# Transposing attention probabilities with the DMA engines instead of TensorE in a fused attention and feed-forward kernel

## The chip, the core and the metric

The kernel runs on one core of a Trainium2 chip. The core has five engines with an instruction queue each: TensorE (PE in the profile; its weight loads are PEld), VectorE (DVE), ScalarE (ACT), GpSimd (POOL) and SyncE (SP), which here issues the DMA transfers. An engine takes its instructions in order, and waits for other engines and for transfers by semaphores. The metric is the device time of one execution in microseconds.

## The reference

Attention over 4 batches of 8 heads, 768 positions and 64 numbers per head; each position sees the first `n_global` = 8 keys and the `n_local` = 96 keys that end with itself, with a bias that falls with the distance. The heads' outputs, side by side, are the 3072 rows of 512 numbers that go into a gated feed-forward layer with 1536 inner columns.

```python
scores = scale * np.matmul(q, k.transpose(0, 1, 3, 2))
keep = is_global | is_local
scores = np.where(keep, scores + bias[None], -1000000000.0)
a = np.exp(scores - np.max(scores, axis=-1, keepdims=True))
a = a / (np.sum(a, axis=-1, keepdims=True) + 1e-09)
x = np.matmul(a, v)                       # then heads side by side
gate = 1.0 / (1.0 + np.exp(-(x @ w_gate)))
out = (gate * (x @ w_val)) @ w_out
```

## The kernel before

The 3072 rows are worked on in 8 blocks of 384 rows (3 tiles of 128), two per batch; `PAIR` is 1, so blocks 0 and 1 come first in a prologue, and "the third block" is block 2. The feed-forward layer of a block takes 12 slices, one for each 128 of the 1536 inner columns, 96 slices in all. A slice (`ff_in`, then `ff_out` of the slice before) is: 12 matmuls into the bank ps_g (L537), a tanh on ACT that makes the gate (L545), 12 matmuls into ps_u, a multiplication on DVE that empties ps_u (L554), the split of the product into a rounded part hh (ACT) and a rest hl (DVE), and 9 output matmuls into ps_o (L577). A number is multiplied as a rounded part plus a rest; so the slice's output weights are split too, w2h on ACT (L217) and w2l on POOL (L180).

While the feed-forward layer of a block runs, the attention of the next block is put between its instructions. An attention item is one tile of 128 rows for one pair of heads: 12 per block, 4 pairs (steps) of 3 tiles. An item goes through these stages:

- S, `scores`: matmuls into ps_s (L387 for blocks 2 and on), bias and minimum on DVE (L406), exponential on ACT (L419); the result, 128 rows by 2 heads by 256 key columns in 32 bits, is a tile work. At the first tile of a batch the rows have 128 key columns.
- T, `normalise` and `transposes`: DVE divides by the sums (L434 to L438), PE transposes 128x128 pieces into the bank ps_t (L449; 4 pieces, 2 at the first tile of a batch), and one copy brings them to the SBUF tile pT (ACT at L457, for two thirds of block 0 DVE at L455).
- V, `values`: for both pairs of two steps together, matmuls of pT with v (L476), after which ACT and DVE write the split x of the next block (xh L518, xl L519).

A list of events gives each stage its slice: S at slice u, T at u + 1, V at u + 1 of the last tile of a step, with u spread over the slices of the block before. Events of kind 0 run ahead of `ff_in`, of kind 1 in its middle, behind the gate, of kind 2 behind it, ahead of `ff_out`. A scheduler then orders each engine's queue by its own estimates of time; `issue_after` holds one instruction behind another of the same engine. The inputs of a step are loaded two steps ahead (L301 to L325), into buffers that the step before last must have freed; SP issues loads and output stores (L600) in one order.

Of the kernel before, what the change touches and what calls it, by code (L numbers as in the profile page):

```python
# [8 lines left out]
F32 = mybir.dt.float32  # L9
# [3 lines left out]
I16 = mybir.dt.int16  # L13
# [6 lines left out]
P = 128  # L20
# [8 lines left out]
def attn_moe_kernel(ctx, tc, qT, kT, v, n_global, n_local, wg, wv, wo, out, B, H, S, D):  # L29
    nc = tc.nc  # L30
    DM = H * D
    NC = DM // P
    NF = wo.shape[0] // P
# [2 lines left out]
    TB = 3  # L36
    NB = TB * P
    WORKB = 4
    OSTB = 4
    PTB = 3  # L40
    QB = 2
    SCALE = 1.0 / float(D) ** 0.5
# [13 lines left out]
    spool = inner.enter_context(tc.tile_pool(name="spool", bufs=2))  # L56
# [3 lines left out]
    late = {}  # L60

    def issue_after(later, earlier):
        tc.add_manual_dep(
            later.ins,
            earlier.ins.name,
            mybir.DependencyInfo(mybir.DependencyClass.NoSync, mybir.DependencyReason.DATA),
            reason="issue order",
        )
# [5 lines left out]
    words = cpool.tile([P, 2, 2], I32, name="words")  # L74
# [74 lines left out]
    last_gate = []  # L149
# [118 lines left out]
    PAIR = 1  # L268
# [15 lines left out]
    steps = {}  # L284
# [66 lines left out]
    def bank(*names):  # L351

        i = turns.get(names, 0)
        turns[names] = i + 1
        name = names[i % len(names)]
        pool = {"ps_s": ps_a, "ps_t": ps_a, "ps_v": ps_a, "ps_g": ps_gv, "ps_u": ps_gv}.get(name, ps_o)
        return pool.tile([P, 4 * P], F32, name=name)
# [82 lines left out]
    def transposes(bi, s, t):  # L440
        st = steps[bi, s]
        b, t0, nt = blocks[bi]
        n = 1 if t0 + t == 0 else 2
        sb, _ = st.pop(("s", t))
        pt = bank("ps_t", "ps_o0") if bi < PAIR else bank("ps_t")
        pt = pt.rearrange("p (c x) -> p c x", c=4)
        for j in range(2):
            for c in range(n):
                nc.tensor.transpose(pt[:, n * j + c], sb[:, j, c * P:(c + 1) * P], ident)  # L449
        if bi > PAIR and s % 2:  # L450
            pT = late["pool"].tile([P, 4, P], F32, name="pT2", bufs=PTB)
        else:
            pT = spool.tile([P, 4, P], F32, name="pT", tag="pT", bufs=PTB)
        if bi < PAIR and t > 0:
            nc.vector.tensor_copy(pT[:, 0:2 * n], pt[:, 0:2 * n])  # L455
        else:
            nc.scalar.copy(pT[:, 0:2 * n], pt[:, 0:2 * n])  # L457
        st["pT"][t] = pT

    def values(bi, pairs):  # L460
        b, t0, nt = blocks[bi]
        n = nt * P

        lead = None
        avs = []
        for s in reversed(pairs):
            st = steps.pop((bi, s))
            shared = bi == PAIR or (bi > PAIR and s % 2)
            av = ps_a.tile([P, 4 * P], F32, name="ps_t" if shared else "ps_v")
            avs.append((s, av, st))  # L470
            for t in reversed(range(nt)):
                vts = (st["v1"],) if t0 + t == 0 else (st["v0"], st["v1"])
                m = len(vts)
                for c, vt in enumerate(vts):
                    for j in range(2):
                        ins = nc.tensor.matmul(  # L476
                            av[j * D:(j + 1) * D, t * P:(t + 1) * P],
                            vt[:, t, j * D:(j + 1) * D],
                            st["pT"][t][:, m * j + c],
                            start=(c == 0),  # L480
                            stop=(c == m - 1),
                        )
                        if lead is not None:
                            issue_after(ins, lead)
                        lead = ins
        for s, av, st in avs:
            pair_out(bi, s, av, st)
# [33 lines left out]

    outs = {}
    hs = {}

    UNSPLIT = 8

# [34 lines left out]
    def ff_out(bi, f):  # L561
        b, t0, nt = blocks[bi]
        if bi < PAIR and f < UNSPLIT:
            (h,) = hs.pop((bi, f))
            parts = ((h, w2f[f].bitcast(F32)),)
        else:
            hh, hl = hs.pop((bi, f))
            held, wh, wl = w2[0]
            assert held == f
            parts = ((hh, wl), (hh, wh), (hl, wh))  # L570
        if f == 0:
            outs[bi] = [ps_o.tile([P, DM], F32, name=f"ps_o{i}") for i in range(nt)]
        end = f == NF - 1 and bi == nblk - 1
        before = None
        for t in range(nt):
            for k, (ht, wt) in enumerate(parts):
                ins = nc.tensor.matmul(  # L577
                    outs[bi][t],
                    ht[:, t * P:(t + 1) * P],
                    wt,  # L580
                    start=(f == 0 and k == 0),
                    stop=(f == NF - 1 and k == len(parts) - 1),
                )

                if end and before is not None:
                    issue_after(ins, before)
                before = ins
        if f == NF - 1:
            for t in range(nt):
                ot = late["pool"].tile([P, DM], F32, name="ost", bufs=OSTB)  # L590
                if t == nt - 1 and end:
                    half = slice(0, DM // 2), slice(DM // 2, DM)
                    nc.scalar.activation(ot[:, half[0]], outs[bi][t][:, half[0]], AF.Copy, scale=0.5)  # L593
                    nc.vector.tensor_scalar(ot[:, half[1]], outs[bi][t][:, half[1]], 0.5, None, op0=ALU.mult)  # L594
                elif t == 1 and end:
                    nc.vector.tensor_scalar(ot, outs[bi][t], 0.5, None, op0=ALU.mult)
                else:
                    nc.scalar.activation(ot, outs[bi][t], AF.Copy, scale=0.5)
                row = b * S + (t0 + t) * P
                nc.sync.dma_start(out[bass.ds(row, P), :], ot)  # L600
# [8 lines left out]
    for bi, (b, t0, nt) in enumerate(blocks):  # L609
        items = [(s, t) for s in range(NPAIR) for t in range(nt)]  # L610
        if bi < PAIR:
            w = (-200, -80)
        elif bi == PAIR:
            w = (0, NF - LEAD)
        else:

            w = ((bi - 1) * NF - (LEAD if bi > PAIR + 1 else 0), bi * NF - LEAD)
        for k, (s, t) in enumerate(items):
            u = w[0] + k * (w[1] - w[0]) // len(items)

            lag = AHEAD if bi < PAIR else 1
            events.append((u, 0, "S", bi, s, t))
            events.append((u + lag, 1, "T", bi, s, t))
            if t == nt - 1:
                events.append((u + lag * (1 if bi >= PAIR else 2), 1 if bi == PAIR else 2, "V", bi, s, t))
    order = sorted(range(len(events)), key=lambda i: (events[i][0], events[i][1], i))
    events = [events[i] for i in order]

# [9 lines left out]
    def run(kind, bi, s, t):  # L638
        if kind == "S":
            if t == 0 and (bi, s) == (0, 0):  # L640
                ready_step((bi, s))
            scores(bi, s, t)
            if t == blocks[bi][2] - 1:
                i = all_steps.index((bi, s))
                if i + 1 < len(all_steps) and all_steps[i + 1] != (PAIR + 1, 0):
                    ready_step(all_steps[i + 1])
        elif kind == "T":
            normalise(bi, s, t)
            transposes(bi, s, t)
        else:  # L650
            if bi <= PAIR:
                values(bi, (s,))
            elif s % 2:
                values(bi, (s - 1, s))
# [18 lines left out]
        pos += 1  # L673
    prev = None
    for u, (bi, f) in enumerate(seq):
        group = {0: [], 1: [], 2: []}
        while pos < len(events) and events[pos][0] <= u:
            group[events[pos][1]].append(events[pos][2:])
            pos += 1
        if bi == 0:  # L680
            conv_until(2 * f)
        if u == NF - LEAD:
            conv_until(len(conv))
            cstack.close()
            late["pool"] = inner.enter_context(tc.tile_pool(name="late", bufs=1))
            load_step(PAIR + 1, 0)
            ready_step((PAIR + 1, 0))
        for e in group[0]:
            run(*e)
        if bi == 0:  # L690
            conv_step()

        def mid(es=group[1]):
            for e in es:
                run(*e)
            if bi == 0:
                conv_step()

        ff_in(bi, f, mid)
        for e in group[2]:  # L700
            run(*e)
        if prev is not None:
            ff_out(*prev)
        if bi < PAIR:
            conv_until(2 * f + 1)
        if bi >= PAIR or f >= UNSPLIT:
            split_w2(f, u == len(seq) - 1)
        prev = (bi, f)
# [149 lines left out]
```

## Time and profile before

| | |
|---|---|
| median of 3 runs | 769.31 us (768.39 to 769.98) |
| the profiled execution, its time | 771.78 us |
| its span, first to last instruction | 770.0 us |
| mean granted TensorE clock | 0.990 |
| PE busy, weight loads | 755.6 us (98%), 682.3 us (89%) |
| DVE, ACT, POOL busy | 405.6, 408.8, 213.2 us |
| DMA moved | 57.01 MB, mean 74 GB/s |

In a row of groups, the parts are: line, engine, operation, tile written <- tiles read, shape, count, then total busy us and mean ns of one, then the idle time of the engine ahead of them with what ended it. In a row by stretches, they are: the stretch in us, its length, then busy us and count for PE, PEld, DVE, ACT and POOL (or those that the chosen tile has), the granted clock, the busy share of the DMA engines and GB/s. In a row in order of time: start, duration, engine, line, operation, tiles, count, and in brackets the idle time ahead. A row of DMA issues ends with KB each and the median us from issue to landing. A row of waits gives who waited for whom: us in total, times, longest.

### The profile page before, as it was taken

The numbers are of one execution on the slowest core, as the hardware profiler recorded it, in microseconds if no ns is written. First come the engines' busy times: TensorE is split into PE (matmuls) and PEld (weight loads), VectorE is DVE, ScalarE is ACT, GpSimd is POOL, SyncE is SP. The second block draws the span as 40 slices with busy tenths as digits, with TensorE's granted clock in tenths as the row PEclk, the third lists the DMA queues.
The fourth block names the chain that finished last, engine by engine and source line by source line (L and its number), as shares of the span: only waits on it lengthen the run. The fifth ranks groups of instructions, "written<-read, shape, count | busy, mean of one in ns | idle before, by whom it ended". The sixth has DMA issues, their size and how long they took to land. (4 is left out here: it accounts for less than half of the span.)

```text
span 770.0 us, 12641 instructions
## 1 busy us (share of the span) xinstructions
PE 755.6 (98%) x4661; PEld 682.3 (89%) x4661; DVE 405.6 (53%) x1085; ACT 408.8 (53%) x944; POOL 213.2 (28%) x164
## 2 busy tenths in 40 slices
PE   8999999999999999999999999999999999999996
PEld 5767678899999999999999999999999999999995
DVE  6789887556445555554565544454654565221111
ACT  4689876645546555553556554464555555432222
POOL 5424234332313323221232322222221222112222
PEclk7999999999999999999999999999999999999998
DMA  8768553403022121122113110221211200000001
GB/s 255 218 214 263 179 194 91 120 14 92 8 73 77 34 75 33 39 83 58 37 37 92 60 54 20 68 74 37 71 37 42 78 25 17 1 10 33 1 0 46
DMA packets 66982, 57.01 MB, mean 74 GB/s; under 512 B 17248, under 2 KB 59232, under 8 KB 66912
## 3 DMA queue, kind: packets, MB, share of 16 engines
q1 hardware_dynamic: 66912, 56.12, 24.7%
q8 instruction: 39, 0.64, 0.3%
q14 instruction: 31, 0.25, 0.1%
HBM read 49.81 MB, written 6.29 MB: 73 GB/s over the span
## 5 line engine op out<-in xcount | busy, mean ns | idle before, releaser
L180 POOL TENSOR_TENSOR w2l<-w2f,w2h 128x512 fp32r<-128x512 f32 x87 | 114.0, 1310 | 414.3 <-ACT w2h L217 406.3
L554 DVE SCALAR_TENSOR_TENSOR work<-work,ps_u 128x384 f32<-128x384 f32 x88 | 48.7, 553 | 216.7 <-PE ps_u L537 207.8
L537 PE MATMUL ps_u<-xh,w1l 128*128 128x384 f32 x384 | 134.4, 350 | 0.0
L537 PE MATMUL ps_g<-xh,w1l 128*128 128x384 f32 x384 | 131.3, 342 | 1.2 <-ACT work L545 1.2
L537 PE MATMUL ps_g<-xl,w1h 128*128 128x384 f32 x384 | 130.4, 339 | 0.7 <-DVE xl L519 0.7
L537 PE MATMUL ps_u<-xl,w1h 128*128 128x384 f32 x384 | 129.9, 338 | 0.0
L537 PE MATMUL ps_g<-xh,w1h 128*128 128x384 f32 x384 | 129.9, 338 | 0.0
L537 PE MATMUL ps_u<-xh,w1h 128*128 128x384 f32 x384 | 129.9, 338 | 0.0
L557 ACT ACTIVATE hh<-work 128x384 fp32r<-128x384 f32 x88 | 46.0, 522 | 128.0 <-DVE work L554 128.0
L419 ACT ACTIVATE work<-work,nms 128x256 f32<-128x256 f32 (+1 forms) x192 | 92.0, 481 | 27.4 <-DVE nms L406 27.0
L577 PE MATMUL ps_o<-w2l,hh 128*128 128x512 f32 x261 | 104.7, 401 | 0.7 <-POOL w2l L180 0.6
L577 PE MATMUL ps_o<-w2h,hh 128*128 128x512 f32 x261 | 102.7, 394 | 0.0
L577 PE MATMUL ps_o<-w2h,hl 128*128 128x512 f32 x261 | 102.6, 394 | 0.0
L217 ACT ACTIVATE w2h<-w2f 128x512 fp32r<-128x512 f32 x87 | 54.9, 631 | 89.6 <-PE ps_o L577 88.6
L180 DVE TENSOR_TENSOR hl<-work,hh 128x384 fp32r<-128x384 f32 x88 | 69.3, 788 | 28.9 <-ACT hh L557 28.7
L537 PEld LDWEIGHTS ps_g<-xh,w1l 128*128 128x128 f32 x384 | 72.3, 188 | 5.2 <-issue 2.6
L537 PEld LDWEIGHTS ps_g<-xl,w1h 128*128 128x128 f32 x384 | 72.2, 188 | 3.0 <-DVE xl L519 1.1
L537 PEld LDWEIGHTS ps_u<-xh,w1l 128*128 128x128 f32 x384 | 72.3, 188 | 1.1 <-issue 0.2
L537 PEld LDWEIGHTS ps_u<-xl,w1h 128*128 128x128 f32 x384 | 72.4, 189 | 0.5
L537 PEld LDWEIGHTS ps_g<-xh,w1h 128*128 128x128 f32 x384 | 72.2, 188 | 0.7
L537 PEld LDWEIGHTS ps_u<-xh,w1h 128*128 128x128 f32 x384 | 72.2, 188 | 0.2 <-issue 0.2
L406 DVE CUSTOM_DVE_ANT_0 work<-ps_s,tab 128x256 f32<-128x256 f32 x136 | 52.7, 420 | 25.4 <-PE ps_s L387 25.0
(131 smaller groups left out, 1169.1 us busy)
## 6 DMA issues: line engine op xcount, KB each, us to landing
qr<-in_qT SPq DMA_DIRECT2D x56, 192.0 KB, 3.3
kr<-in_kT SPq DMA_DIRECT2D x32, 192.0 KB, 2.6
v<-in_v SPq DMA_DIRECT2D x32, 192.0 KB, 3.1
raw<-in_w_gate SPq DMA_DIRECT2D x12, 512.0 KB, 4.2
raw<-in_w_val SPq DMA_DIRECT2D x12, 512.0 KB, 5.8
raw<-in_w_out SPq DMA_DIRECT2D x12, 512.0 KB, 3.8
out<-ost SPq DMA_DIRECT2D x24, 256.0 KB, 2.2
v<-in_v SPq DMA_DIRECT2D x16, 144.0 KB, 2.7
```

The costliest lines, as they stand in the source:

```text
L180: eng.tensor_tensor(out, a, b, op=ALU.subtract)
L217: ins = nc.scalar.activation(hi, w, AF.Copy)
L406: ins = nc.vector.tensor_tensor_reduce(sb[:, j, :w], ps[j][:, :w], (tabs0 if zero else tabs)[2 * s + j], -SCALE, 3.0e38, op0=ALU.add, op1= ...
L419: ins = nc.scalar.activation(sb[:, j, :w], sb[:, j, :w], AF.Exp, scale=-1.0, bias=nm[:, j:j + 1], accum_out=sm[:, j:j + 1])
L537: nc.tensor.matmul(ps[:, :n], wt[f][:, i, c], xt[:, c, :n], start=(k == 0), stop=(k == 3 * NC - 1))
L554: nc.vector.scalar_tensor_tensor(a[:, :n], a[:, :n], 1.0, pss[1][:, :n], op0=ALU.add, op1=ALU.mult)
L557: nc.scalar.activation(hh[:, :n], a[:, :n], AF.Copy)
L577: ins = nc.tensor.matmul(outs[bi][t], ht[:, t * P:(t + 1) * P], wt, start=(f == 0 and k == 0), stop=(f == NF - 1 and k == len(parts) - 1),)
```

## The change

From block 2 on, T no longer uses PE. `transposes_by_dma` takes the 32-bit probabilities as 16-bit halves: two DVE copies (L467) put the lower halves and the upper halves of all pieces side by side in one tile `halves` (one buffer, 128 x 1024, or 128 x 512 at the first tile of a batch), and a transposing DMA on SP's queue (L469) writes `turned` (two buffers). A new stage J, `join`, runs one slice later: an ACT copy (L482) writes the lower halves and a DVE copy (L483) the upper halves into pT, each held behind that slice's gate tanh on its list of events. V moves to u + 2 of the last tile, behind `ff_out`, and its matmuls are held behind the last output matmul. The events of block 2 spread over 9 slices in place of 10, and those of the later blocks start and end one slice earlier. The output tiles `ost` have 3 buffers in place of 4. The values that are computed stay the same.

```diff
-    OSTB = 4
+    OSTB = 3
...
         sb, _ = st.pop(("s", t))
+        if bi > PAIR:
+            st["pT"][t] = transposes_by_dma(s, n, sb)
+            return
         pt = bank("ps_t", "ps_o0") if bi < PAIR else bank("ps_t")
...
-        if bi > PAIR and s % 2:
-            pT = late["pool"].tile([P, 4, P], F32, name="pT2", bufs=PTB)
-        else:
-            pT = spool.tile([P, 4, P], F32, name="pT", tag="pT", bufs=PTB)
+        pT = spool.tile([P, 4, P], F32, name="pT", tag="pT", bufs=PTB)
...
+    def transposes_by_dma(s, n, sb):
+
+        m = 2 * n
+        halves = late["pool"].tile([P, 2 * 4 * P], I16, name="halves")[:, 0:2 * m * P]
+        words = sb[:, :, 0:n * P].bitcast(I16).rearrange("p j (x h) -> p j x h", h=2)
+        for h in range(2):
+            dst = halves[:, h * m * P:(h + 1) * m * P].rearrange("p (j x) -> p j x", j=2)
+            nc.vector.tensor_copy(dst, words[:, :, :, h])
+        turned = late["pool"].tile([P, 2 * 4, P], I16, name="turned", bufs=2)[:, 0:2 * m]
+        nc.sync.dma_start_transpose(turned, halves)
+        return turned
+
+    def join(bi, s, t):
+        st = steps[bi, s]
+        turned = st["pT"][t]
+        m = 2 if blocks[bi][1] + t == 0 else 4
+        if s % 2:
+            pT = late["pool"].tile([P, 4, P], F32, name="pT2", bufs=PTB)
+        else:
+            pT = spool.tile([P, 4, P], F32, name="pT", tag="pT", bufs=PTB)
+        words = pT[:, 0:m].bitcast(I16).rearrange("p c (x h) -> p c x h", h=2)
+
+        issue_after(nc.scalar.copy(words[:, :, :, 0], turned[:, 0:m]), last_gate[-1])
+        issue_after(nc.vector.tensor_copy(words[:, :, :, 1], turned[:, m:2 * m]), last_gate[-1])
         st["pT"][t] = pT
...
-        lead = None
+        lead = last_out[-1] if bi > PAIR else None
...
+        last_out[:] = [before]
...
-            w = ((bi - 1) * NF - (LEAD if bi > PAIR + 1 else 0), bi * NF - LEAD)
+            w = ((bi - 1) * NF - (LEAD + 1 if bi > PAIR + 1 else 0), bi * NF - LEAD - 1)
...
+            if bi > PAIR:
+                events.append((u + 2 * lag, 1, "J", bi, s, t))
             if t == nt - 1:
-                events.append((u + lag * (1 if bi >= PAIR else 2), 1 if bi == PAIR else 2, "V", bi, s, t))
+                after, kind = (2, 2) if bi < PAIR else (1, 1) if bi == PAIR else (2, 3)
+                events.append((u + after * lag, kind, "V", bi, s, t))
...
         if prev is not None:
             ff_out(*prev)
+        for e in group[3]:
+            run(*e)
```

How the queues change is seen in three places. First TensorE, in a slice of the next to last block (w1l_153 and w1h_141 are the weights of one slice). Before, between the gate matmuls and the output matmuls, and the same once more behind the output matmuls:

```order
L537 MATMUL ps_g<-xh,w1h_141 128x384
L449 MATMUL ps_t<-ident,work 128x128 x2
L577 MATMUL ps_o_6696<-w2l,hh 128x512
L577 MATMUL ps_o_6696<-w2h,hh 128x512
L577 MATMUL ps_o_6696<-w2h,hl 128x512
```

Now, at the same place:

```order
L564 MATMUL ps_g<-xh,w1h_141 128x384
L604 MATMUL ps_o_6804<-w2l,hh 128x512
L604 MATMUL ps_o_6804<-w2h,hh 128x512
L604 MATMUL ps_o_6804<-w2h,hl 128x512
L604 MATMUL ps_o_6805<-w2l,hh 128x512
```

The transposes are gone from the queue, here and behind the output matmuls, and nothing stands in their place. The value matmuls, which stood ahead of a slice's output matmuls every sixth slice, now stand behind them.

Second VectorE, from the multiplication that empties ps_u to the next one, in a slice without a split of k. Before:

```order
L554 SCALAR_TENSOR_TENSOR work<-work,ps_u 128x384
L406 ISA work,nms<-ps_s,tab_127 128x256
L406 ISA nms 128x1
L406 ISA work,nms<-ps_s,tab_128 128x256
L406 ISA nms 128x1
L180 TENSOR_TENSOR hl<-work,hh 128x384
L434 TENSOR_SCALAR sm<-sm 128x2
L436 RECIPROCAL rc<-sm 128x2
L438 TENSOR_SCALAR work<-work,rc 128x256 x2
L554 SCALAR_TENSOR_TENSOR work<-work,ps_u 128x384
```

Now:

```order
L581 SCALAR_TENSOR_TENSOR work<-work,ps_u 128x384
L406 ISA work,nms<-ps_s,tab_125 128x256
L406 ISA nms 128x1
L406 ISA work,nms<-ps_s,tab_126 128x256
L406 ISA nms 128x1
L180 TENSOR_TENSOR hl<-work,hh 128x384
L434 TENSOR_SCALAR sm<-sm 128x2
L436 RECIPROCAL rc<-sm 128x2
L483 COPY pT_6936<-turned 128x512
L438 TENSOR_SCALAR work<-work,rc 128x256 x2
L467 COPY halves<-work 128x512 x2
L581 SCALAR_TENSOR_TENSOR work<-work,ps_u 128x384
```

The join of the item before stands ahead of the normalising, and the two copies into halves behind it; all three stand ahead of the next multiplication. In other slices the join stands between the normalising and the copies, or behind them.

Third SyncE's queue, around the first items of block 6. Before:

```order
L309 DMA kr<-in_kT 128x3x128
L310 DMA kr<-in_kT 128x2x32
L305 DMA qr<-in_qT 64x2x384 x2
L324 DMA v_5123<-in_v 96x2x128
L320 DMA v_5124<-in_v 128x3x128
L325 DMA v_5123<-in_v 32x2x128
L324 DMA v_5349<-in_v 96x2x128
```

Now:

```order
L309 DMA kr<-in_kT 128x3x128
L310 DMA kr<-in_kT 128x2x32
L305 DMA qr<-in_qT 64x2x384 x2
L324 DMA v_5133<-in_v 96x2x128
L320 DMA v_5134<-in_v 128x3x128
L325 DMA v_5133<-in_v 32x2x128
L469 DMA_TRANSPOSE turned<-halves 128x8x128
L320 DMA v_5363<-in_v 128x3x128
L324 DMA v_5362<-in_v 96x2x128
L325 DMA v_5362<-in_v 32x2x128
L469 DMA_TRANSPOSE turned<-halves 128x4x128
```

A transposing transfer now stands behind loads of v, and loads of v behind it, in the one order in which SP issues. There are 72 such transfers, one for each item of blocks 2 to 7.

More of the change, by code (lines that the diff above doesn't have):

```diff
@@ L458, in transposes @@
         st["pT"][t] = pT
+    def transposes_by_dma(s, n, sb):
[19 more added lines that the diff above has]
+        issue_after(nc.vector.tensor_copy(words[:, :, :, 1], turned[:, m:2 * m]), last_gate[-1])
+        st["pT"][t] = pT
     def values(bi, pairs):
@@ L523, in attn_moe_kernel @@
     hs = {}
+    last_out = []
     UNSPLIT = 8
@@ L649, in run @@
             transposes(bi, s, t)
+        elif kind == "J":
+            join(bi, s, t)
         else:
@@ L675, in attn_moe_kernel @@
     for u, (bi, f) in enumerate(seq):
-        group = {0: [], 1: [], 2: []}
+        group = {0: [], 1: [], 2: [], 3: []}
         while pos < len(events) and events[pos][0] <= u:
```

## The prediction

> **What bounds the kernel now.** I read the page's shares first, then the engines by stage, then TensorE in order of time inside one slice of the feed-forward loop.
>
> ```profile
> PE 755.6 (98%) x4661; PEld 682.3 (89%) x4661; DVE 405.6 (53%) x1085; ACT 408.8 (53%) x944; POOL 213.2 (28%) x164
> 192.00:668.00 476.00, 476.00 (x3003) 445.05 (x3002) 246.61 (x691) 248.67 (x599) 121.42 (x83) 1.00 0.18 50
> 192.00:668.00 476.00, 73.22 (x186) 34.90 (x186) 53.46 (x63) 0.00 (x0) 1.00 0.18 50
> ```
>
> The second row is the stretch 192 to 668 us: PE 476.00 of 476 us, DVE 246.61, ACT 248.67, POOL 121.42, granted clock 1.00, DMA share 0.18. The third is the same stretch for the tile hl alone: 186 of its output matmuls, three to a slice, so 62 slices of 476 / 62 = 7.68 us. TensorE never stops; VectorE has 246.61 / 62 = 3.98 us of work per slice. Busy time cannot tell what one matmul is worth, because their spans overlap, so I go by starts:
>
> ```profile
> 434.21 0.34 PE L537 MATMUL ps_g<-xl,w1h 128*128 128x384 f32 x1
> 434.38 0.34 PE L537 MATMUL ps_g<-xh,w1h 128*128 128x384 f32 x1
> 434.56 0.49 PE L449 MATMUL ps_t<-ident,work 128*128 128x128 f32 x3
> 434.80 0.48 PE L577 MATMUL ps_o<-w2l,hh 128*128 128x512 f32 x1
> 435.12 0.39 PE L577 MATMUL ps_o<-w2h,hh 128*128 128x512 f32 x1
> 435.35 0.40 PE L577 MATMUL ps_o<-w2h,hl 128*128 128x512 f32 x1
> ...
> 436.73 0.39 PE L577 MATMUL ps_o<-w2h,hl 128*128 128x512 f32 x1
> 436.96 0.27 PE L449 MATMUL ps_t<-ident,work 128*128 128x128 f32 x1
> 436.99 0.42 PE L537 MATMUL ps_u<-xh,w1l 128*128 128x384 f32 x1
> 437.25 0.34 PE L537 MATMUL ps_u<-xl,w1h 128*128 128x384 f32 x1
> ...
> 440.02 0.64 PE L387 MATMUL ps_s<-ks,qs 128*128 128x256 f32 x4
> ...
> 444.14 0.42 PE L537 MATMUL ps_u<-xh,w1l 128*128 128x384 f32 x1
> ```
>
> A gate matmul starts every 0.17 us, an output matmul every 0.23. From the last gate matmul (434.38) to the second output matmul (435.12) are 0.74 us; without the three transposes it would be 0.17 + 0.23 = 0.40. Three transposes cost 0.34, or 0.113 each. The single one: 436.73 to 437.25 is 0.52 against 0.23 + 0.17, so 0.12. Four are 0.45 of the 7.15 us between 436.99 and 444.14. PE is bound by its own queue, so what leaves it comes off the end.
>
> **What the change removes.**
>
> ```profile
> L449 PE MATMUL ps_t<-ident,work 128*128 128x128 f32 x332 | 54.6, 277 | 0.0
> L449 PE MATMUL ps_o<-ident,work 128*128 128x128 f32 x20 | 4.1, 317 | 0.6 <-ACT pT L457 0.6
> L457 ACT COPY pT<-ps_t 128x512 f32<-128x512 f32 (+1 forms) x86 | 46.6, 542 | 8.0 <-PE ps_t L449 8.0
> L192 ACT ACTIVATE w2f<-raw 128x512 int32<-128x512 uint32 x12 | 8.0, 664 | 1.7 <-DMA raw<-in_w_out 1.7
> ```
>
> 332 + 20 = 352 transposes run now. Blocks 0 and 1 keep 88 (2 x 4 head pairs x 3 tiles x 4, less 2 in each of the 4 first tiles of block 0); 264 go. 264 x 0.113 = **29.8 us** off the PE queue: per item 264 / 72 = 3.67, or 0.41 us, which takes the mean slice from 7.68 to 7.27. On ACT, one PSUM copy (0.54) is replaced by one strided 16-bit copy, nearest the strided 128x512 row at 0.66: +0.1 us beside 4.0 of 7.27, which is covered by idle time.
>
> **What it adds to VectorE.** Three 16-bit copies per item: two that part the words, one that joins. Nothing of this kind runs now. The nearest rows, both strided 16-bit with 512 elements, bound it:
>
> ```profile
> L203 DVE TENSOR_SCALAR neg<-raw 128x512 int16<-128x512 int16 x12 | 6.8, 568 | 0.0
> L214 DVE SCALAR_TENSOR_TENSOR w2f<-top,w2f 128x512 int16<-128x512 int16 x12 | 14.4, 1201 | 2.3 <-ACT w2f L192 1.5
> L438 DVE TENSOR_SCALAR work<-work,rc 128x256 f32<-128x256 f32 x144 | 53.1, 408 | 2.3
> L180 DVE TENSOR_TENSOR hl<-work,hh 128x384 fp32r<-128x384 f32 x88 | 69.3, 788 | 28.9 <-ACT hh L557 28.7
> L554 DVE SCALAR_TENSOR_TENSOR work<-work,ps_u 128x384 f32<-128x384 f32 x88 | 48.7, 553 | 216.7 <-PE ps_u L537 207.8 <-PE ps_t L719 5.2 <-ACT work L545 3.6
> 435.39 1.90 DVE L180 TENSOR_TENSOR hl<-work,hh 128x384 fp32r<-128x384 f32 x1 [0.30 <-ACT hh L557]
> 435.02 1.86 POOL L180 TENSOR_TENSOR qs<-qr,qs 128x768 fp32r<-128x768 f32 x1 [2.96 <-ACT qs L345]
> ```
>
> I take 0.57 (one input, as the new copies), with 1.20 as the dear end. DVE's work rises to 3.98 + 3 x 0.57 = 5.69 of 7.27 us: 78%. The last two rows show a DVE subtraction stretched to 1.90 us while POOL subtracts beside it, so lateness of an us or so must be expected; who minds is read here:
>
> ```profile
> 439.43 0.56 DVE L554 SCALAR_TENSOR_TENSOR work<-work,ps_u 128x384 f32<-128x384 f32 x1 [1.21 <-PE ps_u L537]
> 442.08 0.47 ACT L545 ACTIVATE work<-ps_g 128x384 f32<-128x384 f32 x1
> 443.47 0.62 DVE L438 TENSOR_SCALAR work<-work,rc 128x256 f32<-128x256 f32 x2
> 444.38 0.63 ACT L217 ACTIVATE w2h<-w2f 128x512 fp32r<-128x512 f32 x1 [1.34 <-PE ps_o L577]
> ```
>
> The new copies stand ahead of the multiplication that empties ps_u. It begins at 439.43; PE writes ps_u again at 444.14: about 4 us of cover, less 0.45. Cheap copies are hidden. Where they are not: the third block has 12 items in 9 slices, 1.33 each. An item is (3.98 - 0.79 - 0.55) + 1.71 = 4.35 us there, with hl (0.79) and that multiplication (0.55) once per slice, so 1.33 x 4.35 + 1.34 = 7.1 us against a PE slice near 7.3, with nothing to spare. My estimate is 2 us lost there, and 2 us for all late moments elsewhere.
>
> **The transfer.** Each item sends 256 KB (128 KB for a first tile) from SBUF to SBUF, transposing. No transfer of that kind is in the trace. The rows:
>
> ```profile
> out<-ost SPq DMA_DIRECT2D x24, 256.0 KB, 2.2
> v<-in_v SPq DMA_DIRECT2D x32, 192.0 KB, 3.1
> qr<-in_qT SPq DMA_DIRECT2D x56, 192.0 KB, 3.3
> kr<-in_kT SPq DMA_DIRECT2D x16, 32.0 KB, 2.3
> raw<-in_w_val SPq DMA_DIRECT2D x12, 512.0 KB, 5.8
> q1 hardware_dynamic: 66912, 56.12, 24.7%
> SPq L324 <- PE ps_t L476: 135.1, 12, 26.9
> ```
>
> Low end 2.2 us from issue to landing, like 256 KB of output; high end 5.8, the slowest row. Between: if every run of 128 halves (256 bytes) is a packet, 1024 packets over 16 engines at q1's mean of 0.247 x 16 x 770 us / 66912 = 45 ns make 2.9 us on top of the 2.3 that 32 KB take, 5.2 without any overlap. I take 3.8.
>
> What it may take: the halves exist at 443.47 + 0.62 + 1.14 = 445.2. In the next slice ACT's gate ends at 442.08 + 0.47 + 7.27 = 449.8, and behind it stands the join; behind the join stands w2h, which waits for PE until 444.38 + 7.27 = 451.7 anyway. A landing of 4.5 us delays nothing, 5.8 (451.7 less 0.66, less 445.2) not yet w2h. In VectorE's order the joins stand ahead of the normalising in 23 of the regular slices, between it and the halves in 13, behind the halves in 24. There is one halves buffer, so a turn costs L + 2.53 (0.57 + 2 x 0.41 + 2 x 0.57), L + 1.71 or L + 1.14: L + 1.8 in the mean. At 3.8 that is 5.6, and 6.3 in the strictest order, both under 7.27; the third block's 1.33 turns make 7.5 a slice, 2 us lost in its 9. At 5.8 it is 7.6: 72 x 0.33 = 24 us lost, most of the gain. At 2.2 nothing is lost.
>
> [...]
>
> **Sum.** The profiled execution took 771.78 us, span 770.0. Stalls: 2 + 2 + 2 = 6 us. Span: 770.0 - 29.8 + 6 = 746.2; with the 1.8 around it 748. The median of the runs is 2.5 lower (769.31), so **745 us**.
>
> **The rivals.**
>
> *The transfer bounds the loop* (slower). Place: halves wait for the transfer before, joins for theirs, and behind both on DVE waits the multiplication that frees ps_u. It decides from L = 7.68 - 1.8 = 5.9 us. If packets are half the size that I assumed, L is 2.3 + 5.8 = 8.1, a turn 9.9, and the time 769.3 + 72 x (9.9 - 7.68) = 929. For it: no such row, many small pieces. Against it: DMA engines 18% busy in the stretch, and plain rows of this size at half the limit. [...] Chance 0.23, spread from 775 upwards.
>
> *VectorE takes PE's place.* With copies at 1.20, as L214, DVE needs 3.98 + 3.60 = 7.6 us, the old slice: 62 x 0.3 = 20 us of the gain go, time about 765. For it: POOL's interference and L214. Against it: L214 has two inputs. Chance 0.12 (0.07 still faster, 0.05 the same).
>
> *SyncE's order.* Transposes now stand in one queue with loads that wait for buffers; the last row above shows loads of v waiting up to 26.9 us for the value matmuls. If in each of 12 pairs of steps a transpose waits one such load (3.1 us to land) past its cover, 12 x 3 = 36 us are lost: 776. Against it: these loads are placed after the matmuls that release them. Chance 0.07.
>
> **How the numbers follow.** Forecast 0.58 (its own range 738 to 752: no stall at all is 769.3 - 29.8 = 739.5; twice the stalls 751), the others as given. Within 0.2% (1.5 us, about what a measurement tells from no change) only part of the second rival falls: 0.05. Faster 0.58 + 0.07 = 0.65; slower 0.23 + 0.07 = 0.30. Range 738 to 805: it takes in both smaller rivals and the near part of the first; what is over 805, L above about 6.4, is under 0.2.
>
> **What would show it.** Right: 88 transposes on PE, PE near 100% between 192 and 640 us, slices of 7.27 us, transposes landing within 4.5 us, DVE near 78%, copies of 0.4 to 0.7 us. Wrong: idle PE before ps_u or ps_t matmuls, DVE halves or ACT joins that wait for the DMA, landings above 5.9 us, copies above 1 us.

## The result and the profile after

The changed kernel takes 744.94 us (median of four runs, 744.80 to 747.63), the kernel before 769.64 (768.39 to 772.38) beside it: a ratio of 0.968, interval 0.966 to 0.970. The forecast was 745. The profiled execution of the change has a span of 743.1 us, that of before 770.0.

The page of the changed kernel, first its busy times, then its main DMA queue (packets, MB, share of 16 engines), and from the DMA view the row of the new transfers (size of one not given; median us from issue to landing):

```profile
PE 725.0 (98%) x4397; PEld 654.6 (88%) x4397; DVE 499.2 (67%) x1301; ACT 417.5 (56%) x944; POOL 214.4 (29%) x164
...
q1 hardware_dynamic: 136800, 73.43, 39.8%
...
turned<-halves SPq DMA_TRANSPOSE x72, 3.1
```

264 instructions have left TensorE (4661 to 4397), which is as full as it was: 98%. VectorE has risen from 53% to 67%. The new transfers land in 3.1 us. The groups of instructions, with equal lines kept in one row, show the new copies:

```profile
L467 DVE COPY halves<-work 128x512 int16<-128x512 int16 (+1 forms) x144 | 63.2, 481 | 18.6 <-DMA turned<-halves 17.1
L482 ACT COPY pT<-turned 128x512 int16<-128x512 int16 (+1 forms) x72 | 51.5, 722 | 2.8 <-DMA turned<-halves 2.8
L452 PE MATMUL ps_t<-ident,work 128*128 128x128 f32 x68 | 11.4, 282 | 0.0
```

Only VectorE's halves wait for transfers in any amount: 17.1 us.

To place the gain I cut both executions into the same stretches: the program's first 116 us, the attention of the third block (block 2, the first with the new path), and that of the fourth to the seventh. A stretch of a block ends where ScalarE begins to copy a block's output. The windows view gives start and end, length, busy time and number of instructions of PE, PEld, DVE, ACT and POOL, granted clock, DMA share and GB/s. Before:

```profile
0.00:116.00 116.00, 109.40 (x656) 80.37 (x658) 93.84 (x241) 87.05 (x188) 45.61 (x49) 0.96 0.71 220
143.70:237.40 93.70, 93.70 (x587) 87.62 (x586) 52.91 (x149) 52.14 (x130) 26.28 (x17) 1.00 0.22 59
237.40:603.00 365.60, 365.60 (x2315) 341.86 (x2314) 192.20 (x537) 192.08 (x465) 93.88 (x64) 1.00 0.20 55
```

And after:

```profile
0.00:116.00 116.00, 107.73 (x680) 80.04 (x681) 97.38 (x246) 88.97 (x194) 47.29 (x51) 1.00 0.72 220
141.30:235.60 94.30, 91.19 (x552) 84.19 (x551) 73.42 (x206) 54.14 (x136) 26.07 (x17) 1.00 0.48 99
235.60:579.80 344.20, 344.20 (x2122) 322.16 (x2121) 251.70 (x673) 197.45 (x463) 94.56 (x64) 1.00 0.40 92
```

The four blocks of the last row take 344.2 us instead of 365.6, and TensorE idles in neither. The third block takes 94.3 instead of 93.7, though it too has lost its transposes: TensorE now idles 3.1 us there. The first stretch has no new path; the profiled execution of before had a clock of 0.96 there, against 1.00. The same cut for every profiled execution (us; each boundary is the start of the first output copy on ScalarE in the timeline):

| kernel | third block | 4th | 5th | 6th | 7th | 8th | five together |
|---|---|---|---|---|---|---|---|
| before | 93.7 | 91.7 | 91.8 | 92.0 | 90.1 | 88.0 | 453.6 |
| after | 94.3 | 85.5 | 85.8 | 87.0 | 85.8 | 84.8 | 428.9 |
| transposes put back | 95.7 | 92.2 | 90.4 | 91.7 | 90.4 | 89.0 | 453.7 |
| rest of the change alone | 93.7 | 92.0 | 90.5 | 92.0 | 90.6 | 89.1 | 454.2 |
| transfer twice | 112.3 | 101.8 | 93.7 | 96.4 | 99.4 | 85.1 | 476.4 |
| small transfer ahead | 109.2 | 85.1 | 87.9 | 85.4 | 90.7 | 82.9 | 432.0 |
| halves copied twice | 106.3 | 85.9 | 85.4 | 87.4 | 85.4 | 85.1 | 429.2 |
| joins in the same slice | 94.0 | 87.1 | 85.8 | 87.0 | 85.8 | 84.8 | 430.5 |
| third block a slice longer | 88.5 | 87.0 | 85.8 | 87.1 | 85.8 | 84.8 | 430.5 |
| the same, and two halves buffers | 85.4 | 87.0 | 85.8 | 87.0 | 85.8 | 84.7 | 430.3 |
| two halves buffers | 88.9 | 87.0 | 85.8 | 87.0 | 85.8 | 84.7 | 430.3 |
| two halves buffers, end mended | 88.9 | 87.0 | 85.8 | 87.0 | 85.8 | 84.7 | 430.3 |
| transfer twice, two buffers | 100.7 | 87.0 | 85.8 | 87.0 | 85.8 | 84.8 | 430.4 |
| halves copied twice, two buffers | 91.9 | 86.6 | 85.4 | 87.5 | 85.4 | 85.2 | 430.1 |

A boundary can fall a few matmuls earlier or later in TensorE's queue from one kernel to the next: after the change the third block counts 552 matmuls and the five others 2643, with two halves buffers 544 and 2651. Eight feed-forward matmuls are about 1.5 us (by the starts of the working, 0.17 us apart for 24 of a slice and 0.23 for 9), so a single cell says no more than that, and sums over blocks are firmer.

From before to after, the five blocks give 453.6 - 428.9 = 24.7 us for 60 items with 224 transposes: 0.110 us each. (All six blocks of the version with two halves buffers give 28.2 for 264, or 0.107.) The third block should have given 40 x 0.113 = 4.5 and took 0.6 more, so by this cut 5.1 us went there; TensorE is seen idle for 3.1 us there. The rest of the difference of the two spans (26.9) is 2.4 at the start, where the clock was lower before, and 0.4 at the end. Without the start it is 24.5, which agrees with the difference of the medians, 24.7.

Inside a slice the gain is seen by starts. TensorE's timeline, the four score matmuls of one slice and those of the next, first before the change:

```profile
417.65 0.64 PE L387 MATMUL ps_s<-ks,qs 128*128 128x256 f32 x4
...
424.81 0.64 PE L387 MATMUL ps_s<-ks,qs 128*128 128x256 f32 x4
```

And after it:

```profile
418.72 0.64 PE L387 MATMUL ps_s<-ks,qs 128*128 128x256 f32 x4
...
425.49 0.65 PE L387 MATMUL ps_s<-ks,qs 128*128 128x256 f32 x4
```

From one to the other are 7.16 us before and 6.77 after: 0.39 less, for four transposes. VectorE's timeline of the slice after the change:

```profile
422.26 0.45 DVE L483 COPY pT<-turned 128x512 int16<-128x512 int16 x1
422.60 0.60 DVE L438 TENSOR_SCALAR work<-work,rc 128x256 f32<-128x256 f32 x2
423.23 0.77 DVE L467 COPY halves<-work 128x512 int16<-128x512 int16 x2
425.76 0.56 DVE L581 SCALAR_TENSOR_TENSOR work<-work,ps_u 128x384 f32<-128x384 f32 x1 [1.76 <-PE ps_u L564]
```

The three copies are done at 424.00, and the multiplication that frees ps_u still waits 1.76 us for TensorE: the cover was there.

The third block is another matter. VectorE's timeline there, with the end of one item and the halves of the next (in brackets the idle time before, and who ended it):

```profile
198.99 1.76 DVE L467 COPY halves<-work 128x512 int16<-128x512 int16 x2
...
208.79 0.76 DVE L467 COPY halves<-work 128x512 int16<-128x512 int16 x2 [3.56 <-DMA turned<-halves]
```

SyncE's queue between them:

```profile
201.57 0.39 SPq L309 DMA_DIRECT2D kr<-in_kT  x1
202.02 0.47 SPq L310 DMA_DIRECT2D kr<-in_kT  x1
202.54 0.48 SPq L315 DMA_DIRECT2D kr<-in_kT  x1
203.11 0.63 SPq L305 DMA_DIRECT2D qr<-in_qT  x1
203.92 1.25 SPq L469 DMA_TRANSPOSE turned<-halves  x1
```

The halves were complete at 200.75, and the transfer left at 203.92, behind four loads. (It also landed late: the next halves went on 4.9 us after it left, where 3.1 is the median.) The first of the loads had waited for the K buffer that VectorE was still reading. SyncE's waits within the third block (total us, times, longest) have that wait in their second row:

```profile
SPq L469 <- DVE halves L467: 21.2, 7, 3.9
SPq L309 <- DVE ks L180: 14.3, 3, 7.0
```

VectorE's halves wait eight times for a transfer there, 15.7 us in all. Before four of these waits (2.43, 2.00, 3.56 and 2.01 us, 10.0 together) the transfer had left 2.9 to 4.9 us after its halves were complete, behind loads that waited there or were being issued. The other four waits (5.7 us) had none of this.

What TensorE itself waits for in the third block (matmuls alone):

```profile
PE ps_s L387 <- DVE ks L180: 1.8, 1, 1.8
PE ps_o L604 <- POOL w2l L180: 0.7, 1, 0.7
PE ps_u L564 <- DVE work L581: 0.5, 1, 0.5
```

The longest wait, 1.8 us up to 201.60, is for a split of K that stands behind the halves of 198.99 in VectorE's queue. VectorE came to it late for two reasons that the trace shows: it had waited 2.00 us for a transfer at 194.47, and the pair of copies at 198.99 took 1.76 us, 1.0 longer than most.

### The profile page after: what moved, and what is told of

Read it like the earlier page. It is cut to its first block, busy times and chain, and to the rows that moved or that the text cites. A ratio compares the mean times of both kernels' runs of the same rounds, so it can differ in the third digit from the quotient of the medians.

```text
span 743.1 us, 12458 instructions
## 1 busy us (share of the span) xinstructions
PE 725.0 (98%) x4397; PEld 654.6 (88%) x4397; DVE 499.2 (67%) x1301; ACT 417.5 (56%) x944; POOL 214.4 (29%) x164
## 2 busy tenths in 40 slices
DMA packets 136871, 74.32 MB, mean 100 GB/s; under 512 B 87136, under 2 KB 129120, under 8 KB 136800
## 3 DMA queue, kind: packets, MB, share of 16 engines
q1 hardware_dynamic: 136800, 73.43, 39.8%
## 5 line engine op out<-in xcount | busy, mean ns | idle before, releaser
L180 POOL TENSOR_TENSOR w2l<-w2f,w2h 128x512 fp32r<-128x512 f32 x87 | 117.3, 1348 | 377.8 <-ACT w2h L217 363.2
L564 PE MATMUL ps_u<-xh,w1l 128*128 128x384 f32 x384 | 131.3, 342 | 0.6 <-DVE work L581 0.5
L604 PE MATMUL ps_o<-w2l,hh 128*128 128x512 f32 x261 | 102.3, 392 | 0.8 <-POOL w2l L180 0.7
L180 DVE TENSOR_TENSOR hl<-work,hh 128x384 fp32r<-128x384 f32 x88 | 74.4, 845 | 22.3 <-ACT hh L584 22.2
L467 DVE COPY halves<-work 128x512 int16<-128x512 int16 (+1 forms) x144 | 63.2, 481 | 18.6 <-DMA turned<-halves 17.1
```

The source lines that it names most:

```text
L180: eng.tensor_tensor(out, a, b, op=ALU.subtract)
L467: nc.vector.tensor_copy(dst, words[:, :, :, h])
L564: nc.tensor.matmul(ps[:, :n], wt[f][:, i, c], xt[:, c, :n], start=(k == 0), stop=(k == 3 * NC - 1))
L604: ins = nc.tensor.matmul(outs[bi][t], ht[:, t * P:(t + 1) * P], wt, start=(f == 0 and k == 0), stop=(f == NF - 1 and k == len(parts) - 1),)
```

## The experiments

Each edit is against the changed kernel.

**Does the gain come from TensorE's queue?** The 264 transposes are issued again, into a PSUM bank that nobody reads; the new path works as in the change.

```diff
         if bi > PAIR:
+            pt = bank("ps_t").rearrange("p (c x) -> p c x", c=4)
+            for j in range(2):
+                for c in range(n):
+                    nc.tensor.transpose(pt[:, n * j + c], sb[:, j, c * P:(c + 1) * P], ident)
             st["pT"][t] = transposes_by_dma(s, n, sb)
```

> The changed kernel with the 264 TensorE transposes put back into the queue of blocks 2 to 7, writing a bank that nobody reads; the DMA path still does the work. If the gain is the freed places in the TensorE queue (theory A), 264 x 0.113 = 29.8 us come back: 770 to 776. If the gain comes from the rest of the change (other order of the value matmuls, fewer PSUM reads, other windows; rival), it stays below 752.

Measured: 770.58 us, ratio to before 0.9996 (0.9975 to 1.0016). The five blocks are back at 453.7, and TensorE is busy in all of them, so the transposes cost their places in its queue and not a wait. All of the gain is in the queue slots of TensorE.

**Does anything else in the change gain?** The new path is taken out: TensorE transposes and ScalarE copies as before. The 9 slices of block 2, the earlier windows and the 3 output buffers stay as in the change, and the value matmuls stand behind the output matmuls of their slice, though one slice earlier than in the change.

```diff
-        if bi > PAIR:
-            st["pT"][t] = transposes_by_dma(s, n, sb)
-            return
...
-        pT = spool.tile([P, 4, P], F32, name="pT", tag="pT", bufs=PTB)
+        if bi > PAIR and s % 2:
+            pT = late["pool"].tile([P, 4, P], F32, name="pT2", bufs=PTB)
+        else:
+            pT = spool.tile([P, 4, P], F32, name="pT", tag="pT", bufs=PTB)
...
-                after, kind = (2, 2) if bi < PAIR else (1, 1) if bi == PAIR else (2, 3)
+                after, kind = (2, 2) if bi < PAIR else (1, 1) if bi == PAIR else (1, 3)
...
-            join(bi, s, t)
+            pass
```

> The rest of the change alone: TensorE transposes and the ACT copy as before, but block 2 in 9 slices, later blocks one slice earlier, 3 output buffers, and the value matmuls behind the output matmuls of their slice. Theory A: no gain, 767 to 773. Rival (the rest of the change makes the gain): 745 to 755.

Measured: 771.83 us, 1.0018 (0.9996 to 1.004). Nothing is gained without the removal.

**Is there a landing time from which the loop is bound by the turn?** Every transfer is made twice, one after the other, into the same tile.

```diff
         nc.sync.dma_start_transpose(turned, halves)
+        nc.sync.dma_start_transpose(turned, halves)
```

> Each transposing transfer is made twice into the same tile, the second after the first has landed, so the landing takes 2 x 3.1 = 6.2 us. Theory A (a turn of halves, transfer, join and normalising takes the landing plus 1.1 to 2.5 us by the order of the slice, 1.8 in the mean, and is free while under the slice of 7.27 us): 8.0 us per turn, 72 x 0.7 = 53 us slower than the changed kernel, 790 to 805, with the halves copies waiting for the DMA. Rival (the transfer is hidden with room to spare, since joins stand a slice later): under 752.

Measured: 811.86 us, 1.0528 (1.0485 to 1.0571), over the end of the range. VectorE's waits over the whole program have one large row, and its timeline in the fifth block shows one of them:

```profile
DVE halves L467 <- DMA turned<-halves: 159.0, 59, 6.9
```

```profile
403.40 0.49 DVE L467 COPY halves<-work 128x256 int16<-128x256 int16 x2 [4.92 <-DMA turned<-halves]
```

The first of the two transfers before it left SyncE at 396.83, the second at 400.24, and the halves went on at 403.40: a landing of 6.6. The five blocks take 476.4 / 60 = 7.94 us per item, which is the 6.6 plus 1.4: a turn within the working's L + 1.14 to L + 2.53. Of the 47.5 us that the five blocks lose against the change, TensorE is idle for 31.3; its granted clock there is 0.98 against 1.00, and what the rest is, the run does not show. What I had missed is the third block, 18 us longer than in the change.

**The same question near the limit.** A transfer of one 128x128 block goes ahead of each, into a place that the large one then overwrites.

```diff
+        nc.sync.dma_start_transpose(turned[:, 0:1], halves[:, 0:P])
         nc.sync.dma_start_transpose(turned, halves)
```

> Ahead of each transposing transfer a small one of 128x128 halves into the same tile, which must land first (estimate 2.4 us, the shortest landing seen): the landing takes about 5.5 us. Theory A: a turn takes 7.3 us in the mean and 8.0 in the strictest order, so the slices begin to stretch: 750 to 765. Rival (hidden anyway): under 748. Rival (any turn over the slice in any order counts in full): above 775.

Measured: 768.34 us, 0.996 (0.9933 to 0.9987); over the range again, and again through the third block. At a landing of 5.5 (399.85 to 405.37 in its timeline) the five blocks lose 3.1 us, the third 14.9; TensorE is idle for 11.7 us in the third block, against 3.1 in the change, at a granted clock of 0.95 against 1.00. With the doubled transfer this puts the landing at which the regular blocks are as slow as before (453.6) between 5.5, where they take 432.0, and 6.6, where they take 476.4; the working had 5.9.

**What does more VectorE work cost?** The copies into halves are made twice.

```diff
             nc.vector.tensor_copy(dst, words[:, :, :, h])
+            nc.vector.tensor_copy(dst, words[:, :, :, h])
```

> The two DVE copies into halves are each made twice: 2 x 0.52 = 1.04 us more VectorE work per item. Theory A (VectorE has room except in the dense third block): 4 to 12 us slower, nearly all of it while block 2's attention runs. Rival (VectorE has become the bound together with TensorE): 72 x 1.04 = 75 us slower, near 820.

Measured: 758.21 us, 0.9843 (0.9808 to 0.9878): 13 slower than the change, over the 4 to 12 expected. The windows of the third block and of the five others:

```profile
141.95:248.20 106.25, 94.56 (x553) 86.01 (x552) 79.41 (x234) 53.59 (x134) 25.89 (x17) 0.98 0.39 88
248.20:677.50 429.30, 428.92 (x2642) 400.85 (x2641) 345.39 (x908) 236.75 (x553) 115.77 (x78) 1.00 0.38 82
```

In the five, VectorE is busy 345.39 of 429.30 us, 80%, and TensorE loses 0.4. The third block takes the whole loss, 12 us.

**Is it the one halves buffer there?** A second one; to make room, one output buffer fewer.

```diff
-    OSTB = 3
+    OSTB = 2
...
-        halves = late["pool"].tile([P, 2 * 4 * P], I16, name="halves")[:, 0:2 * m * P]
+        halves = late["pool"].tile([P, 2 * 4 * P], I16, name="halves", bufs=2)[:, 0:2 * m * P]
```

> Two buffers for halves (and 2 output buffers in place of 3, for the room). In the changed kernel DVE waited 15.7 us for the DMA before it could write halves, nearly all between 130 and 240 us, where the block lasts 94.3 us and the later ones 85 to 87. Theory A (the one buffer costs the third block its gain): 2 to 5 us faster than the changed kernel, 740 to 743. Rival (VectorE's work itself, 75 of 97 us busy there, or late joins, cost it): within 1 us of the changed kernel.

Measured: 743.26 us, 0.9659 (0.9635 to 0.9683), just over the range and not told apart from the change. The third block becomes 5.4 us shorter and the fourth 1.5 longer. That 1.5 is the eight matmuls that the boundary between them has moved, so the buffer is worth some 4 us; 2.3 are given back behind the last block, where the output now waits for a buffer (9.8 us from the last boundary to the end of the span, against 7.5; ScalarE's copy of the last output tile waits 3.1 us, against 0.8).

**Is it the pace of items there?** The third block's window is begun a slice earlier: 10 slices for its 12 items, not 9.

```diff
-            w = ((bi - 1) * NF - (LEAD + 1 if bi > PAIR + 1 else 0), bi * NF - LEAD - 1)
+            w = ((bi - 1) * NF - (LEAD + 1 if bi > PAIR + 1 else 1), bi * NF - LEAD - 1)
```

> Block 2's attention starts one slice earlier and has 10 slices in place of 9 for its 12 items; all else as changed. Theory A (the third block lost its gain because 1.33 turns do not fit a slice): 2 to 4 us faster than the changed kernel, 741 to 743. Rival (it was lost to the loads and splits of the first step, which come as late as before): within 1 us.

Measured: 747.37 us, 0.9702 (0.9677 to 0.9727), no gain. The third block becomes 5.8 us shorter, and the work ahead of it ends 6.6 later (147.96 instead of 141.34), but most of this is work that has changed sides: 25 more matmuls come ahead of the boundary (856 against 831). TensorE's idle time shows what was gained: 3.2 us in the third block, as in the change (3.1), and 11.2 ahead of it instead of 8.8, spread over several short waits. So the slower pace took none of the idle time away, and the earlier start added 2.4 us of it. Both edits together:

> Both: 10 slices for block 2, and two buffers for halves with 2 output buffers. Theory A: 3 to 6 us faster than the changed kernel, 739 to 742. If one edit alone removes the loss, the same as the better of the two.

Measured: 745.17 us, 0.9678 (0.9654 to 0.9702). Missed as well. TensorE is idle 0.4 us in the third block, thanks to the buffer, and 10.8 ahead of it, through the earlier start.

**The second buffer, with the end mended.** As with two buffers, and the last tile of the last block takes a buffer of the work pool, which is idle by then.

```diff
-                ot = late["pool"].tile([P, DM], F32, name="ost", bufs=OSTB)
+                if t == nt - 1 and end:
+                    ot = mpool.tile([P, DM], F32, name="work", tag="work", bufs=WORKB)
+                else:
+                    ot = late["pool"].tile([P, DM], F32, name="ost", bufs=OSTB)
```

> Two buffers for halves and 2 output buffers as in the earlier run, but the last tile of the last block is brought out through a free work tile, so that the end does not wait for a store. The earlier run was 4 to 5 us ahead of the changed kernel at the start of the last block's end and gave 2.3 us back behind it. Theory A: 740 to 742, 3 to 5 us faster than the changed kernel. Rival (the difference between those profiles was noise of the start): 743 to 745.

Measured: 741.04 us (740.10 to 742.12), 0.961 (0.9585 to 0.9634): the best version, within the expected range and some 4 us under the change. Its windows of the third block and of the next four:

```profile
142.40:231.20 88.80, 88.69 (x544) 82.86 (x543) 70.52 (x206) 54.97 (x135) 26.82 (x17) 1.00 0.50 106
231.20:577.00 345.80, 345.80 (x2131) 323.64 (x2130) 251.60 (x673) 197.84 (x463) 94.25 (x64) 1.00 0.40 91
```

TensorE is full in the third block, which takes 88.8: the 93.7 of before less the 4.5 of its transposes, and nothing lost. SyncE's waits in that block have not gone, as their row for the K loads shows:

```profile
SPq L309 <- DVE ks L180: 11.8, 3, 5.9
```

The transfers still stand behind loads that wait; what has gone is that VectorE stands behind the transfers. In this block no halves wait for one any more. The scheduler has also ordered VectorE anew: no halves stand between the two parts of a K split there, as they did at 198.99. The run does not part this from the buffer.

**Does the second buffer part landing and VectorE for good?** The doubled transfer on top of this version.

> The transfer made twice (landing 6.2 us), but with two buffers for halves, else as halves2_end. If the single halves buffer couples the landing to VectorE (theory A: copies into halves wait for the transfer before), most of the 67 us that the doubled transfer cost goes away: 745 to 770. If the joins are what comes late (rival: they wait for the landing, and with them the normalising behind them), most of it stays: 785 to 812.

Measured: 752.74 us, 0.9757 (0.9726 to 0.9787). At a landing of 6.6, which cost 47.5 us in the five blocks with one buffer (476.4 - 428.9), they now take 430.4, as at the short landing (430.3): nothing. The third block still loses, 100.7 against 88.9. There the joins wait now; VectorE's and ScalarE's waits in that stretch:

```profile
DVE pT L484 <- DMA turned<-halves: 7.3, 2, 4.3
DVE halves L467 <- DMA turned<-halves: 5.1, 1, 5.1
```

```profile
ACT pT L483 <- DMA turned<-halves: 6.5, 2, 5.0
```

**And doubled copies with two buffers.**

> The doubled copies into halves (1.04 us more VectorE work per item) together with two buffers for halves as in halves2_end. With one buffer they cost 13 us, all in the third block. If they cost because each turn through the single buffer became longer (theory A), with two buffers they cost under 4 us: 742 to 745. If VectorE's work itself fills the third block's slices (rival), 8 us or more stay: 749 to 755.

Measured: 746.40 us (743.15 to 747.88), 0.9683 (0.9648 to 0.9719), between the two expectations. Its profiled execution, the fastest of the four, has the third block at 91.9, 3.0 over the version without doubling. With one buffer the same work cost 12.0. By the profiles three quarters of that loss was the buffer's; by the medians, 5.4 of 13.3 us remain (746.40 against 741.04), so some six tenths. Of the rest I can't say how much is VectorE's time itself.

**Is the one slice of delay needed?** The joins are placed in the slice of their transfer.

```diff
             if bi > PAIR:
-                events.append((u + 2 * lag, 1, "J", bi, s, t))
+                events.append((u + lag, 3, "J", bi, s, t))
```

> The join is put at the end of the slice of its transposing transfer in place of one slice later; all else as changed. Theory A (landing 3.1 us; the queue of VectorE is blocked by a join that comes too early, and there are some 4 us of cover before ps_u is missed): a loss between 0 and 20 us, 745 to 765, with DVE joins that wait for the DMA. Rival (the slice of lag carries the whole gain): 770 or more. Rival (the lag is not needed at all): within 1.5 us.

Measured: 748.08 us, 0.9695 (0.9664 to 0.9725). The joins wait 14.3 us on ScalarE and 13.2 on VectorE over the program, but TensorE minds little: it is busy throughout the five blocks, which take 430.5, about what most versions take. The profiled execution is 4.5 us longer than that of the change, and 3.0 of these lie ahead of the third block; its mean granted clock was 0.992 against 0.999. The medians differ by 3.1 us, at the low end of what was expected, but the two intervals overlap: that the delay is worth anything at this landing is not shown.

## Why the prediction was right, and where not

**What bounds the kernel, and the price of a transpose: right.** 0.113 us by starts was forecast, 0.110 measured over 224 (0.107 over 264 with two halves buffers); the slice became shorter by 0.41 us, as forecast (453.6 - 428.9 over 60), and the transposes put back return the old time. The records give each transpose 0.28 us; reading that, one would have expected 264 x 0.28 = 74 us.

**VectorE: right, a little dear.** 78% was forecast, 251.70 / 344.20 = 73% came out. The copies (taken as 0.57) show in their groups of single shapes:

```profile
L467 DVE COPY halves<-work 128x512 int16<-128x512 int16 x120 | 57.3, 519 | 14.4 <-DMA turned<-halves 13.0
L483 DVE COPY pT<-turned 128x512 int16<-128x512 int16 x60 | 33.7, 564 | 0.0
L482 ACT COPY pT<-turned 128x512 int16<-128x512 int16 x60 | 46.1, 771 | 2.8 <-DMA turned<-halves 2.8
```

So the dear end of 1.20, and with it the rival in which VectorE takes TensorE's place, did not come; and VectorE at 80% cost the regular blocks 0.4 us. ScalarE's join was mis-sized low, 0.77 for this shape against 0.66, covered as said.

**The transfer: right in its bounds, a little dear.** Taken 3.8, came 3.1 (2.4 to 4.8). The guess of 256-byte packets holds: 136800 - 66912 = 69888 packets for 17.3 MB, 248 bytes each. Their price was too high: the queue's busy share rose from 24.7% of 770.0 to 39.8% of 743.1, which is 105.6 us on 16 engines, or an estimate of 24 ns for each packet added, against the 45 taken. So the rival of half-sized packets fell, and with it 929 us. The transposing transfers landed about as fast as plain ones: 3.1 us, against 2.2 to 3.3 for plain loads and stores from 144 to 256 KB in the profile before, and 2.2 to 4.2 in that of the changed kernel. Where a transfer of one 128x128 block went ahead of each large one, it landed in 2.3 us, and the large one, mostly of eight blocks, in 3.1.

**The turn: right in the regular blocks.** The landing of 5.9 from which the transfer was to take the whole gain lies between the two tested, and the doubled transfer's 7.94 per item is a turn of L + 1.4 against the mean of L + 1.8.

**The stalls: right in sum, wrong in parts.** 6 us were charged; by the price of 0.113, 5.1 in the third block and 0.6 in the other five (224 x 0.113 = 25.3 less 24.7) were lost. A second buffer brings back 4.2 of these 5.7 in the six blocks together (519.1 against 523.3). The other 1.5 stay away although TensorE is then full, so they belong to the price of a transpose: 264 x 0.006, the difference of 0.113 and 0.107. The 2 us for late moments elsewhere did not come: TensorE is busy in all of the five blocks. Of the working's two terms for the third block, the one for VectorE's work failed: with the same work and a second buffer TensorE idles 0.1 us there. The one for the turn had the right place and the right resource but not the mechanism. At the measured landing its own formula, 1.33 x (3.1 + 1.8) = 6.5 us per slice, would have lost nothing. VectorE's halves waited for transfers all the same, which the working had named as a sign of being wrong. What made the transfers late in 10.0 of 15.7 us of these waits is SyncE's order, which I had as a rival for the whole kernel at 36 us: loads stand ahead of a transposing transfer. Where a K load waits there for its buffer, the chain runs in a ring: VectorE frees the K buffer, VectorE waits for the transfer, and the transfer stands behind the K load. This much is read from the trace: in the third block the K loads wait 14.3 us for VectorE, and VectorE 15.7 for transfers. The runs show that the second buffer, which opens the ring at VectorE and with which VectorE's queue is ordered anew, takes the loss away; that the ring was the whole cause is argued, since copies stretched beside GpSimd (1.76 us for the pair at 198.99, against 0.77 at most clear of it) made VectorE late as well, and whether loads moved behind the transfer would do as much was not tried. So the forecast met the time partly by luck: terms that were too large (landing, VectorE's work) stood for one that was missing.

**Left open:** how much of the third block's loss is the ring and how much the stretched copies, what lengthens the waits ahead of the third block when its attention begins a slice earlier, and what the 3 to 5 us of doubled copies with two buffers are.

## What to carry to other kernels

Price an instruction of a full engine by the starts of its neighbours with and without it, not by its recorded duration: here that gave 0.113 us, the record 0.28, and 0.110 came off. When a round trip through DMA replaces work inside a loop, count buffers on the way out as well as on the way back: here a single one tied the producer to the landing (VectorE waited 159.0 us for transfers at a landing of 6.6), and a second one made that landing free in the regular blocks, where it had cost 47.5 us. Look for the stretch with more than one item per slice, and for loads in the same issuing queue that wait for what the delayed engine frees.

## What the hardware showed that was not expected

One transposing transfer holds SyncE's queue for 1.2 us, where the K loads hold it for 0.39 to 0.48 in the median. The view of the line that issues it (duration in ns, minimum, median and maximum; start of the first and last):

```profile
L469 SPq DMA_TRANSPOSE turned<-halves x72: 1189/1232/2144, 138.3 to 634.5; - x72
...
DMA to landing us min/median/max: 2.4/3.1/4.8
```

The 72 transfers take 72 x 1.23 = 89 us of the queue.

The length of a transposing transfer set little of its landing here. Where one of 128x128 went ahead of each large one of up to 128x1024, the views of the two issuing lines give, first for the small one:

```profile
DMA to landing us min/median/max: 2.2/2.3/4.4
...
DMA to landing us min/median/max: 2.4/3.1/4.8
```

Eight times the data, in most cases, took 0.8 us longer in the median.

The pair of copies into halves takes 0.75 to 0.77 us in most slices, but 1.76 at 198.99 (shown above), while GpSimd subtracts:

```profile
198.85 1.29 POOL L180 TENSOR_TENSOR w2l<-w2f,w2h 128x512 fp32r<-128x512 f32 x1 [0.50 <-ACT w2h L217]
```

Two more pairs in the third block, of 1.87 and 1.90 us, also lie beside such a subtraction. So it is in the whole program: of the pairs of 128x512 copies that the timeline shows as one row, the ten that run beside a GpSimd subtraction for over 1 us take 1.76 to 1.90 each, and none that is clear of one takes over 0.77. The prediction had shown this for VectorE's own subtractions; that plain copies of 16 bits are stretched as well was not in its working.
